# Four w_out rows per partition in one transfer: a change to how the sixteen DMA engines share a weight matrix

## The chip, the core and the metric

The kernel runs on one core of one Trainium2 chip. The metric is the device time of one execution in microseconds (us); before the change it is 663.49 us, the median of three runs (663.15 to 664.74). One core has a matrix engine (TensorE, "PE" in the profile, with its weight loads as "PEld"), a vector engine (VectorE, "DVE"), an activation engine (ScalarE, "ACT"), GpSimd ("POOL"), and SyncE ("SP"), which here only issues transfers. Sixteen DMA engines move data between the chip's memory and the core's 128-partition scratch memory. Each of the computing engines works through its own instructions in order and waits on semaphores for the others.

## What is computed

One decoding step with four sequences, in bf16: attention over a key and value cache, and a small gated MLP (gMLP) beside it, added together.

```python
x, xn = A_x, layernorm(A_x)                      # x: (4, 1, 640)
q = (xn @ wq) per head                           # 32 heads of 128, 4096 cached positions
o = softmax(q @ k_cache^T * 128**-0.5) @ v_cache # k_cache, v_cache: (4, 32, 4096, 128)
z = gelu(xn @ w_in)                              # w_in: (640, 1728)
z1, z2 = z[..., :864], layernorm(z[..., 864:])
g = w_sp @ z2 + b_sp                             # one position: two scalars
out = x + o @ wo + (z1 * g) @ w_out              # wo: (4096, 640), w_out: (864, 640)
```

The two caches are 134 MB each. Of the 282.6 MB that the kernel moves, w_out is 864 rows of 1,280 bytes, 1.1 MB.

## The kernel before

**Memory.** One large buffer `kv` is cut into five slots of SL = 16,384 bf16 elements per partition (32 KB). A unit of cache (all positions of eight heads of one sequence) is 64 KB per partition, 8 MB in all, and takes two neighbouring slots; sixteen units of K and sixteen of V go through the five slots. `place` says which two: K0 goes to slots 3 and 4, K1 to 0 and 1, K2 to 2 and 3, K3 to 4 and 0, V0 to 1 and 2. Before the cache comes, the same slots hold other things: slot 0 holds wq and the layernorm's scratch, slot 2 everything of the gMLP.

Slot 2 is filled from its start in this order (elements per partition): w_in (8,640), the first FA rows per partition of w_out (FA x 640), the float32 array `z_f` (3,840 elements' room), the bf16 array `z_b` (1,280), and `I4`, a 128x128 float32 matrix of ones and zeros (256 elements' room). With FA = 3 they end at 8,640 + 1,920 + 3,840 + 1,280 + 256 = 15,936, inside the slot.

**The rest of w_out.** What `w_out` doesn't hold goes into `w_words` (DVE clears it first, L128), as three pieces (`PC`): 20, 12 and 8 partitions with several rows each. SP issues the first two, POOL the third, behind a small transfer into a tile `walk` that nothing reads. A piece's partitions are dealt out to 5, 3 and 2 DMA engines, four partitions to each. `w_words` is used again later: `kT_t`, the two buffers into which DVE transposes the keys, lies over the same words.

**Order of the transfers.** SP issues nearly all of them, in program order: wq, w_in, w_out (L126, L127), two pieces (L133), K0, K1, K2, K3 (in halves), then V and K in turns (L181). An issue waits until its slots are free. After the last V come the rows of wo that were left (L189), the last in five cuts.

**The gMLP's chain.** After the layernorm of x, PE computes the queries and z (L338, L339 for the rows in `w_out`, L343 for the pieces), ACT applies gelu, and a chain of small steps runs over all engines: DVE sums (L371, L373), PE spreads the sums with `I4` (L376), then L378, L380, L382, L385, L386, L387, L388, L389, a transpose on DVE (L390), and 40 matmuls with w_out on PE (L403), in twenty chunks of two halves. `I4` is written by POOL at L235, and L376 is its only reader.

**The keys.** `emit_K` transposes an eighth of a K unit on DVE (L425) into one of the two buffers and multiplies it on PE (L436). In the order of DVE, K0's transposes stand behind L390. In the order of the source, the issue of K0's transfer (`load_unit(seq[0])`) stands ahead of the copy at L235. A framework places the waits: each instruction waits for the earlier ones, transfers included, that touch the same bytes, and the framework also sets the order within an engine.

Of the kernel before, what the change touches and what calls it, by code (L numbers as in the profile page):

```python
# [16 lines left out]
def kernel(  # L17
# [19 lines left out]
    nc = tc.nc  # L37
    P = 128
# [3 lines left out]
    DC = D // P  # L42
# [9 lines left out]
    NG = H // HG  # L52
# [1 line left out]
    G = HG * B  # L54
    F2 = B_w_in.shape[1]
    Fh = F2 // 2
    FA = 3
    FR = 17
    nf = FA * P

    PC = ((0, 20, 10, 5), (32, 44, 12, 3), (60, 68, 17, 2))
    f_at = [nf]
    for p0, p1, n, _ in PC:
        f_at.append(f_at[-1] + (p1 - p0) * n)
    assert Fh == f_at[-1]
    FC = FA + FR
    NOUT = A_wo.shape[1]
# [18 lines left out]
    def misc_ps(shape, dtype):  # L86
        misc_ctr[0] += 1
        return ps_m.tile(shape, dtype, tag="misc", name=f"misc{misc_ctr[0]}")
# [5 lines left out]
    n_p = (2 * TC + 1) * 16  # L94
    w_words = const.tile([P, max(2 * NKT + n_p, FR * NOUT // 2)], F32, name="w_words")
    kT_t = w_words[:, 0:2 * NKT].rearrange("p (i n) -> p i n", i=2)
    pT_t = w_words[:, 2 * NKT:2 * NKT + n_p].bitcast(BF16).rearrange("p (j r) -> p j r", r=32)

    def at_slot(i, n, off=0):
        return kv[:, i * SL + off:i * SL + off + n]  # L100
# [22 lines left out]

    w_out = at_slot(2, FA * NOUT, n_in).rearrange("p (c n) -> p c n", c=FA)

    nc.sync.dma_start(out=w_out[:, 0:2], in_=B_w_out[0:2 * P, :].rearrange("(p c) n -> p c n", p=P))  # L126
    nc.sync.dma_start(out=w_out[:, 2:3], in_=B_w_out[2 * P:nf, :].rearrange("(p c) n -> p c n", p=P))  # L127
    nc.vector.memset(w_words[:, 0:FR * NOUT // 2], 0.0)  # L128
    w_rest = w_words[:, 0:FR * NOUT // 2].bitcast(BF16).rearrange("p (c n) -> p c n", c=FR)

    def load_piece(eng, t):
        p0, p1, n, k = PC[t]
        return eng.dma_start(out=w_rest[p0:p1, 0:n].rearrange("p c n -> p (c n)"),  # L133
                             in_=B_w_out[f_at[t]:f_at[t + 1], :].rearrange("(r i c) n -> i r (c n)", i=k, c=n))
# [10 lines left out]
    NB = 32 * FC  # L145
    z_at = n_in + FA * NOUT

# [26 lines left out]
    def load_unit(item):  # L174
        key, u = item
        g, b = divmod(u, B)
        cache = A_k_cache if key == "k" else A_v_cache
        src = cache[b, g * HG:(g + 1) * HG].rearrange("e (m t) d -> (e m) (t d)", t=T)
        c = cuts.get(item, (0, T))
        for t0, t1 in zip(c[:-1], c[1:]):  # L180
            nc.sync.dma_start(out=unit(item, t0, t1), in_=src[:, t0 * Dh:t1 * Dh])  # L181
# [5 lines left out]
    def load_wo(g, c_cuts=(0, HG)):  # L187
        for c0, c1 in zip(c_cuts[:-1], c_cuts[1:]):
            nc.sync.dma_start(out=wo_t[g][:, c0:c1, :], in_=wo_q[g][:, c0:c1, :])  # L189
# [30 lines left out]
    xnT = const.tile([P, DC, 32], BF16)  # L220
# [43 lines left out]
    for q in range(4):  # L264
        nc.gpsimd.tensor_copy(out=SelE[32 * q:32 * q + 32, :, q % 2, :],
                              in_=b8[32 * q:32 * q + 32, 8:8 + HP, None].to_broadcast((32, HP, P // HG)))
# [10 lines left out]
                          in_=ident_f[:].rearrange("p (q x c) -> p q x c", q=2, c=C2))  # L277
# [12 lines left out]
    for hf in range(NH):  # L290
        nc.tensor.matmul(proj[0:32, 0:NO2], lhsT=ident_bf[:XR, 1 - hf:33 - hf],
                         rhs=x_bf[:, hf * NO2:(hf + 1) * NO2], start=(hf == 0), stop=False)
# [4 lines left out]
    for hf in range(2):  # L297
        for c in range(DC):
            for j in range(NG):
                n0 = j * HG * Dh + hf * 512  # L300
                nc.tensor.matmul(q4_ps[32 * j:32 * j + 32, hf * 512:hf * 512 + 512], lhsT=xnT[:, c, :],  # L301
                                 rhs=wq[:, c, n0:n0 + 512], start=(c == 0), stop=(c == DC - 1))
# [14 lines left out]
    w_z = w_in.rearrange("p c (a f) -> p c a f", a=2)  # L317
    z_ps = misc_ps([P, 2, FA, 32], F32)
    zr_ps = misc_ps([P, 2, 256], F32)


    z_in = [[], [], [], []]
    for t, (p0, p1, n, k) in enumerate(PC):
        src = w_z[:, :, :, f_at[t]:f_at[t + 1]]
        for q in range(p0 // 32, (p1 - 1) // 32 + 1):
# [5 lines left out]
                src_q = src  # L331
            z_in[q].append((t, x0 - 32 * q, x1 - 32 * q, src_q))
    z_of = [[sum((x1 - x0) * PC[t][2] for t, x0, x1, _ in z[:m]) for m in range(len(z) + 1)] for z in z_in]
    w_z2 = w_z[:, :, :, 0:2 * P].rearrange("p c a (q j i) -> p c q a i j", q=4, j=32)
    w_z1 = w_z[:, :, :, 2 * P:nf].rearrange("p c a (q j) -> p c q a j", q=4)
    for c in range(DC):
        for q in range(4):
            nc.tensor.matmul(z_ps[32 * q:32 * q + 32, :, 0:2], lhsT=xnT[:, c, :], rhs=w_z2[:, c, q], start=(c == 0), stop=False)  # L338
            nc.tensor.matmul(z_ps[32 * q:32 * q + 32, :, 2], lhsT=xnT[:, c, :], rhs=w_z1[:, c, q], start=False,  # L339
                             stop=(c == DC - 1))  # L340
        for q in range(4):
            for m, (_, _, _, src) in enumerate(z_in[q]):
                nc.tensor.matmul(zr_ps[32 * q:32 * q + 32, :, z_of[q][m]:z_of[q][m + 1]], lhsT=xnT[:, c, :], rhs=src[:, c],  # L343
                                 start=(c == 0 and m == 0), stop=(c == DC - 1 and m == len(z_in[q]) - 1))
# [3 lines left out]
    nc.gpsimd.memset(z_f[:, 0:2, :], 0.0)  # L348
    nc.scalar.activation(out=zT[:, :, 0:FA, :], in_=z_ps[:], func=ACT.Gelu_apprx_tanh)
    for q in range(4):  # L350
        rows = slice(32 * q, 32 * q + 32)
        for m, (t, x0, x1, _) in enumerate(z_in[q]):
            p0, p1, n, k = PC[t]
            z = zr_ps[rows, :, z_of[q][m]:z_of[q][m + 1]]
# [3 lines left out]
            else:  # L358
                for a in range(2):
                    nc.scalar.activation(out=dst[:, a].rearrange("p c (i r) -> p c i r", i=k),  # L360
                                         in_=z[:, a].rearrange("p (r i c) -> p c i r", i=k, c=n), func=ACT.Gelu_apprx_tanh)
# [36 lines left out]
    for f0 in range(0, FC, 4):  # L398
        for hf in range(NH):
            for fc in range(f0, min(f0 + 4, FC)):  # L400
# [3 lines left out]
                                 rhs=(w_out[:, fc] if fc < FA else w_rest[:, fc - FA])[:, hf * NO2:(hf + 1) * NO2],  # L404
                                 start=(fc == 1 and hf == 0), stop=False)
# [11 lines left out]
    def emit_K(u, k):  # L417

        g, b = divmod(u, B)
        hh = first.get(u, 0) ^ (k // 4)  # L420
        qp, kh = k // 2 % 2, k % 2
        t0 = 2 * TC * (2 * hh + qp)
        kw = unit(("k", u), t0, t0 + 2 * TC).bitcast(F32).rearrange("p (t w) -> p t w", w=KW)[:, :, 32 * kh:32 * kh + 32]
        kT = kT_t[:, k % 2]
        nc.vector.transpose(kT.rearrange("p (t r) -> p t r", r=32), kw)  # L425
        if ("S", g) not in state:
            S_new = ps_s.tile([P, 2, TC, M], F32, tag="S", name="S")
            state[("S", g)] = S_new
        S_ps = state[("S", g)]
        kb = kT.bitcast(BF16).rearrange("p (i t e m w) -> p i t e m w", i=2, e=NE, m=M, w=2)  # L430
        w0 = 8 - (b * C2 + hh)
        for w in range(2):
            for i in range(2):
                for e in range(NE):
                    q = 2 * qp + e
                    nc.tensor.matmul(S_ps[32 * q:32 * q + 32, i], lhsT=QZ[:, b, 2 * kh + w, e, w0:w0 + 32],  # L436
                                     rhs=kb[:, i, :, e, :, w], start=(b == 0 and k < 4 and kh == 0 and w == 0),
                                     stop=(b == B - 1 and k >= 4 and kh == 1 and w == 1))
# [89 lines left out]
    def emit_sel(g):  # L528

        ox = misc_ps([P, B, P // HG, HG], F32)  # L530
        nc.tensor.matmul(ox[:].rearrange("p b q c -> p (b q c)"), lhsT=SelX[:].rearrange("p h q -> p (h q)"),  # L531
                         rhs=state["R"][:].rearrange("p b d -> p (b d)"), start=True, stop=True)
        om = ppool.tile([P, B, P // HG, HG], F32, tag="p", name="om")
        nc.vector.tensor_tensor(out=om[:], in0=ox[:], in1=MkQ[:, None, :, None].to_broadcast((P, B, P // HG, HG)), op=ALU.mult)
        state[("om", g)] = om
# [27 lines left out]
    for i, item in enumerate(seq):  # L563
        if i + 1 < len(seq):
            key, u = seq[i + 1]
            load_unit(seq[i + 1])
            if key == "k" and u == 2 * B - 1:
                load_wo(u // B - 1)
        else:
            load_wo(NG - 3)  # L570
            load_wo(NG - 2)
            load_wo(NG - 1, (0, 2, 4, 6, 7, 8))
        key, u = item
        g, b = divmod(u, B)
        if key == "k":
            done = b == B - 1 and g > 0
            for k in range(8):
                emit_K(u, k)
                if done and k == 1:
                    emit_sel(g - 1)  # L580
                if done and k == 2:
                    emit_oT(g - 1)
                if done and k == 5 and g == 1:
                    emit_proj(g - 1)
            if b == B - 1:
                if g < NG - 1:
                    fill_qz(g + 1)
                softmax(g)
        else:
            emit_V(u)  # L590
# [58 lines left out]
```

## Time and profile before

| | |
|---|---|
| median of three runs | 663.49 us (663.15 to 664.74) |
| profiled execution, its own time | 663.36 us |
| span of the profiled execution | 661.6 us |
| DMA rate over the span | 427 GB/s, 282.60 MB in 7276 packets |
| DVE, PE busy | 377.3 us, 281.7 us |
| mean granted TensorE clock | 0.755 of full speed |

The trace lists each DMA packet with queue, start, length and size, but not the DMA engine that moved it. On a busy engine a packet begins about 3 ns before the one ahead of it ends, and every engine moves the same sequence of sizes, so the packets fall into sixteen chains. Packets of 12,800 bytes (first piece) appear on five chains, of 15,360 (second) on three of these five, of 21,760 (third) on two others. Eighteen packets of 16,384 bytes of the queue that the page calls "q8 instruction" go to eight further chains in turn, two or three to each; every one takes 1.07 us and draws out a neighbouring packet by about 0.5 us. One chain has neither. By these chains, in us from the span's start:

| chains | K0's share has landed | K1's share has landed | last share of wo has landed |
|---|---|---|---|
| three, both pieces of SP | 45.07, 45.48, 45.51 | 64.40, 64.80, 64.86 | 658.48, 658.03, 658.24 |
| two, first piece only | 42.90, 42.90 | 62.21, 62.22 | 656.29, 658.42 |
| two, POOL's piece | 44.32, 44.41 | 63.64, 63.73 | 656.93, 657.01 |
| six with two instruction packets | 40.70 to 41.07 | 60.02 to 60.39 | 656.49 to 656.82 |
| two with three instruction packets | 40.99, 42.27 | 60.31, 61.63 | 658.07, 658.28 |
| the one left | 42.15 | 61.47 | 654.85 |

Five of the sixteen, the ones with SP's pieces, also show six gaps of 0.30 us, each with a long packet behind it; between the first packet at 2.2 us and the last share of wo no other engine has a gap over 0.05 us.

How to read the answers below: times are us from the span's start; "out<-in" names the tiles; `x8` is a count; a bracket says how long the engine had been idle and who ended it.

### The profile page before, as it was taken

What the parts mean: (1) busy time and instruction counts of PE and PEld (TensorE: products, weight loads), DVE (VectorE), ACT (ScalarE), POOL (GpSimd) and SP (SyncE); (2) the same over time, 40 slices, a digit from 0 to 9 for tenths busy, and PEclk for the clock granted to TensorE, in tenths of its full rate; (3) what the DMA queues carried; (4) which work ended last, traced back from release to release, by engine and by line L of the source; (5) the groups of instructions that cost most, each with busy time, mean ns of one, the idle gap of its engine ahead of it and who ended that gap; (6) DMA issues with size and microseconds to landing.
All of it is one profiled execution on the core that took longest, in us unless ns stands there. A gap on an engine that the chain in (4) does not pass through costs nothing.

```text
span 661.6 us, 5513 instructions
## 1 busy us (share of the span) xinstructions
PE 281.7 (43%) x2293; PEld 106.9 (16%) x2293; DVE 377.3 (57%) x307; ACT 73.9 (11%) x143; POOL 70.3 (11%) x138
## 2 busy tenths in 40 slices
PE   0445555437052455334435075532606245652236
PEld 0221111112011121111112021110202112120012
DVE  4329989766191758718346196864629175971112
ACT  0300000330100000340200000070110000043200
POOL 3620000030200000130300000030020000003300
PEclk9868879778687697677759677875867778666779
DMA  8999999999999999999999999999999999999997
GB/s 367 458 421 440 425 436 445 436 421 440 421 436 437 444 405 436 441 441 436 433 420 428 437 422 445 442 425 432 432 433 432 433 440 411 446 432 429 423 423 286
DMA packets 7276, 282.60 MB, mean 427 GB/s; under 512 B 929, under 2 KB 1324, under 8 KB 1836
## 3 DMA queue, kind: packets, MB, share of 16 engines
q1 hardware_dynamic: 7112, 282.07, 98.9%
q8 instruction: 18, 0.29, 0.2%
q0 software_dynamic: 112, 0.18, 0.1%
q14 instruction: 6, 0.05, 0.0%
q10 hardware_dynamic: 28, 0.01, 0.0%
HBM read 282.25 MB, written 0.01 MB: 427 GB/s over the span
## 4 chain that ended last, share of the span: by engine, by line
DMA 74%; DVE 12%; issue 11%; PE 2%; ACT 0%; SPq 0%; DVEq 0%; ACTq 0%
DMA kv<-in_A_k_cache_dram 63%; DVE w_words L425 11%; DMA kv<-in_A_v_cache_dram 5%; DMA kv<-in_A_wo_dram 3%; DMA kv<-in_A_wq_dram 3%; PE O L509 1%; DVE w_words L491 0%; PE S L436 0%; DVE Zb L469 0%; DVE m L443 0%; PE last L552 0%; ACT p_bf L485 0%; SPq L189 0%; PE proj L552 0%; PE misc L447 0%
## 5 line engine op out<-in xcount | busy, mean ns | idle before, releaser
L425 DVE STREAM_TRANSPOSE w_words<-kv 128x2048 f32<-128x2048 f32 x128 | 282.8, 2275 | 127.2 <-DMA kv<-in_A_k_cache_dram 127.2
L436 PE MATMUL S<-w_words,QZ 128*32 128x512 bf16 x1024 | 183.3, 490 | 262.5 <-DVE w_words L425 262.5
L436 PEld LDWEIGHTS <-QZ 128*32 128x32 bf16 x1024 | 59.2, 110 | 384.3 <-issue 318.1
L509 PE MATMUL O<-kv,Zb 128*32 128x512 bf16 x1024 | 72.0, 443 | 57.6 <-DMA kv<-in_A_v_cache_dram 51.1
L473 ACT ACTIVATE Zb<-w_words,MkE 32x128 bf16<-32x128 bf16 x120 | 60.9, 508 | 117.2 <-PE O L509 103.3
L518 DVE TENSOR_TENSOR om<-O,Mk 128x512 f32<-128x512 f32 x15 | 10.4, 692 | 92.1 <-PE O L509 92.1
L471 POOL TENSOR_SCALAR Zb<-w_words,MkE 32x128 bf16<-32x128 bf16 x60 | 43.3, 722 | 138.6 <-PE O L509 118.0
L485 ACT ACTIVATE p_bf<-S,negmax 128x1024 bf16<-128x1024 f32 x4 | 4.5, 1114 | 401.5 <-DVE negmax L453 401.5
L509 PEld LDWEIGHTS <-Zb 128*32 128x32 bf16 x1024 | 33.3, 110 | 96.1 <-issue 66.5
L469 DVE TENSOR_SCALAR Zb<-w_words,MkE 32x128 bf16<-32x128 bf16 x76 | 24.9, 327 | 2.3
L411 POOL COPY QZ<-qT 32x32 bf16<-32x32 bf16 x16 | 5.0, 315 | 184.9 <-PE S L436 184.3
L519 DVE TENSOR_REDUCE R<-om 128x128 f32<-128x512 f32 x15 | 15.3, 1020 | 0.5
L496 POOL TENSOR_SCALAR rs<-MkB,rowsum 128x4 f32<-128x4 f32 x4 | 1.2, 296 | 112.2 <-ACT p_bf L485 112.2
L491 DVE STREAM_TRANSPOSE w_words<-p_bf 128x1024 bf16<-128x1024 bf16 (+1 forms) x8 | 9.6, 1240 | 5.9 <-ACT p_bf L485 4.1
L542 POOL MEMSET oT<- 128x66 bf16 x4 | 0.5, 146 | 98.0 <-PE proj L552 98.0
L443 DVE TENSOR_REDUCE m<-S 128x1 f32<-128x1024 f32 x4 | 4.9, 1224 | 6.1 <-PE S L436 6.1
L521 DVE TENSOR_SCALAR R<-O,Mk 128x128 f32<-128x128 f32 x1 | 0.4, 351 | 13.0 <-PE O L509 13.0
L531 PE MATMUL misc<-R,SelX 128*128 128x512 f32 x8 | 4.5, 644 | 7.2 <-DVE R L519 5.5
L301 PE MATMUL q<-kv,xnT 128*32 128x512 bf16 x40 | 4.5, 631 | 6.4 <-DVE xnT L222 6.4
L498 PE MATMUL misc<-rs,SelE 128*128 128x4 f32 x8 | 2.3, 364 | 10.4 <-POOL rs L496 10.4
L552 PE MATMUL proj<-kv,oT 128*8 128x320 bf16 x52 | 5.6, 352 | 1.2 <-DMA kv<-in_A_wo_dram 1.2
L128 DVE MEMSET w_words<- 128x5440 f32 x1 | 4.6, 4592 | 1.9 <-issue 1.9
(107 smaller groups left out, 87.9 us busy)
## 6 DMA issues: line engine op xcount, KB each, us to landing
kv<-in_A_k_cache_dram SPq DMA_DIRECT2D x8, 4096.0 KB, 30.2
kv<-in_A_v_cache_dram SPq DMA_DIRECT2D x1, 6144.0 KB, 28.6
kv<-in_A_wq_dram SPq DMA_DIRECT2D x1, 5120.0 KB, 17.2
kv<-in_A_wo_dram SPq DMA_DIRECT2D x3, 1280.0 KB
kv<-in_B_w_in_dram SPq DMA_DIRECT2D x1, 2160.0 KB, 22.7
kv<-in_A_v_cache_dram SPq DMA_DIRECT2D x1, 2048.0 KB
kv<-in_A_wo_dram SPq DMA_DIRECT2D x3, 320.0 KB, 22.7
kv<-in_B_w_out_dram SPq DMA_DIRECT2D x1, 320.0 KB, 23.0
```

Of the source, the lines that this page charges most:

```text
L411: nc.gpsimd.tensor_copy(out=QZ[r0:r0 + 32, :, :, :, 8 + 8 * hp], in_=qT[32 * g:32 * g + 32, NE * hp:NE * hp + NE].rearrange("p e a b -> p ...
L425: nc.vector.transpose(kT.rearrange("p (t r) -> p t r", r=32), kw)
L436: nc.tensor.matmul(S_ps[32 * q:32 * q + 32, i], lhsT=QZ[:, b, 2 * kh + w, e, w0:w0 + 32], rhs=kb[:, i, :, e, :, w], start=(b == 0 and k < ...
L443: nc.vector.tensor_reduce(out=m1[:], in_=S_ps[:].rearrange("p i t m -> p (i t m)"), axis=AX.X, op=ALU.max)
L469: nc.vector.tensor_scalar(out=dst, in0=src, scalar1=mk, scalar2=None, op0=ALU.mult)
L471: nc.gpsimd.tensor_scalar(out=dst, in0=src, scalar1=mk, scalar2=None, op0=ALU.mult)
L473: nc.scalar.activation(out=dst, in_=src, func=ACT.Copy, scale=mk)
L491: nc.vector.transpose(pT_t[:, j0:j1, :], blocks)
L509: nc.tensor.matmul(O_ps[32 * q:32 * q + 32, :, :], lhsT=Zb[b % 2][:, w].rearrange("p h c -> p (h c)"), rhs=vv[:, w * 4 * Dh:(w + 1) * 4 * ...
L518: nc.vector.tensor_tensor(out=om4[:], in0=O_ps[:], in1=Mk4[:, :, None].to_broadcast((P, 4, Dh)), op=ALU.mult)
L519: nc.vector.tensor_reduce(out=R, in_=om4[:].rearrange("p c d -> p d c"), axis=AX.X, op=ALU.add)
L552: nc.tensor.matmul(dst[0:nb, 0:n1 - n0], lhsT=state[("oT", g)][:, c0:c0 + nb], rhs=wo_t[g][:, c, n0:n1], start=start, stop=stop)
```

## The change

FA goes from 3 to 4 and FR from 17 to 16, so `w_out` takes 512 rows, four per partition, in one transfer instead of two, and the pieces have 4, 12 and 16 rows per partition instead of 10, 12 and 17. All else that counts in FA follows: `w_out` is 2,560 elements per partition instead of 1,920, so `z_f`, `z_b` and `I4` begin 640 elements further on, and the end of `I4` is at 16,576. The z matmuls for the rows in `w_out` are one per chunk of x and quarter instead of two. The second to last tile of wo is loaded in two halves.

```diff
-    FA = 3
-    FR = 17
+    FA = 4
+    FR = 16
...
-    PC = ((0, 20, 10, 5), (32, 44, 12, 3), (60, 68, 17, 2))
+    PC = ((0, 20, 4, 5), (32, 44, 12, 3), (60, 68, 16, 2))
...
-    nc.sync.dma_start(out=w_out[:, 0:2], in_=B_w_out[0:2 * P, :].rearrange("(p c) n -> p c n", p=P))
-    nc.sync.dma_start(out=w_out[:, 2:3], in_=B_w_out[2 * P:nf, :].rearrange("(p c) n -> p c n", p=P))
+    nc.sync.dma_start(out=w_out, in_=B_w_out[0:nf, :].rearrange("(p c) n -> p c n", p=P))
...
-    w_z2 = w_z[:, :, :, 0:2 * P].rearrange("p c a (q j i) -> p c q a i j", q=4, j=32)
-    w_z1 = w_z[:, :, :, 2 * P:nf].rearrange("p c a (q j) -> p c q a j", q=4)
+    w_za = w_z[:, :, :, 0:nf].rearrange("p c a (q j i) -> p c q a i j", q=4, j=32)
     for c in range(DC):
         for q in range(4):
-            nc.tensor.matmul(z_ps[32 * q:32 * q + 32, :, 0:2], lhsT=xnT[:, c, :], rhs=w_z2[:, c, q], start=(c == 0), stop=False)
-            nc.tensor.matmul(z_ps[32 * q:32 * q + 32, :, 2], lhsT=xnT[:, c, :], rhs=w_z1[:, c, q], start=False,
-                             stop=(c == DC - 1))
+            nc.tensor.matmul(z_ps[32 * q:32 * q + 32], lhsT=xnT[:, c, :], rhs=w_za[:, c, q], start=(c == 0), stop=(c == DC - 1))
...
             load_wo(NG - 3)
-            load_wo(NG - 2)
+            load_wo(NG - 2, (0, 4, 8))
             load_wo(NG - 1, (0, 2, 4, 6, 7, 8))
```

## The prediction

> **What bounds the kernel now.** I read the slices of the page first, then the chain of waits, then the opening of the timeline, SP's waits and the packet records.
>
> ```profile
> DMA  8999999999999999999999999999999999999997
> DMA kv<-in_A_k_cache_dram 63%; DVE w_words L425 11%; DMA kv<-in_A_v_cache_dram 5%; DMA kv<-in_A_wo_dram 3%; DMA kv<-in_A_wq_dram 3%; PE O L509 1%; DVE w_words L491 0%; PE S L436 0%; DVE Zb L469 0%; DVE m L443 0%; PE last L552 0%; ACT p_bf L485 0%; SPq L189 0%; PE proj L552 0%; PE misc L447 0%
> ```
>
> The DMA engines are busy in every slice, and the chain is mostly DMA. The sixteen chains of packets have no idle time to speak of between 2.2 us and the last wo share, so the span is the packet time of the slowest DMA engine (its last share lands at 658.48) plus a tail of 661.57 - 658.48 = 3.09 us for the last matmuls, the sum and the store. A change can thus act in two ways: through the bytes of the slowest engine, or by letting the queues run dry. The second asks when each transfer is issued:
>
> ```profile
> 17.95 27.57 DMA kv<-in_A_k_cache_dram
> 45.52 0.03 issue
> ...
> 52.36 2.28 DVE w_words L425
> 54.64 0.02 SPq L181
> 54.66 0.04 issue
> 54.70 0.03 SPq L181
> 54.73 0.03 issue
> 54.76 29.46 DMA kv<-in_A_k_cache_dram
> ```
>
> In this stretch of the chain K0 lands at 45.52, DVE transposes its first half, which frees slot 3, and only then, at 54.7, does SP issue K2. The engines are done with K1 between 60.02 and 64.86, so K2 comes 5.3 us ahead of the first to need it. This margin, less the start of a transfer, is all the cover the opening has.
>
> ```profile
> 16.34 0.45 POOL L235 COPY kv<-I 128x128 f32<-128x128 f32 x1
> ...
> 29.80 0.82 DVE L373 TENSOR_REDUCE st_in<-kv 128x1 f32<-128x640 f32 x1 [0.51 <-POOL kv L372]
> 30.67 0.50 PEld L376 LDWEIGHTS misc<-st_in,kv 128*128 128x128 f32 x2 [5.18 <-DVE st_in L373]
> ...
> 37.77 0.85 DVE L390 STREAM_TRANSPOSE kv<-kv 128x640 bf16<-128x640 bf16 x1 [5.33 <-POOL kv L389]
> 38.67 4.85 PEld L403 LDWEIGHTS <-kv 128*8 128x8 bf16 x40 [7.50 <-DVE kv L390]
> ...
> 39.46 4.41 PE L403 MATMUL proj<-w_words,kv 128*8 128x320 bf16 x33
> ...
> 45.74 17.66 DVE L425 STREAM_TRANSPOSE w_words<-kv 128x2048 f32<-128x2048 f32 x8 [7.12 <-DMA kv<-in_A_k_cache_dram]
> ```
>
> The timeline of the opening: the gMLP's chain is over at 43.87, and DVE then waits for K0 with nothing left before it. So the gMLP is hidden, by 45.74 - 43.87 = 1.9 us.
>
> **The change, part by part.**
>
> *Rows and packets.* From the records: a packet of 10,240 bytes costs 385.5 ns, of 2,560 bytes 99, of 1,280 bytes 52; a line between the first two gives 194 for 5,120 (estimate). All engines: w_out was 8 x 99 + 8 x 52 + 12 (two closing packets of 6) = 1,220 ns, becomes 8 x 194 + 6 = 1,558, +0.34 us. The five with the first piece: four packets of 12,800 (476 ns) become 5,120: -1.13, net -0.79. The two with POOL's piece: 21,760 (805 ns) to 20,480, -0.19, net +0.15. The split of wo's second to last tile: 16 x 194 + 12 against 8 x 385.5 + 6, +0.03 for all. If nothing else happened, the three would end at 657.7, the slowest instruction-loaded engine at 658.28 + 0.37 = 658.65, the new end: +0.2 us.
>
> *Fewer z matmuls, a shorter DVE clear, one issue less on SP.* PE drops 20 matmuls and 20 weight loads of L338 and L339, which all lie between 23.9 and 25.4, under the wait for K0; SP's extra issue (0.92 us) was over before the first packet; the clear shrinks by 6% of 4.6 us and holds back only the pieces. Nothing, as long as the wait for K0 is there. One more DMA issue for wo (0.3 us on SP) has 13 us of queued data in front of it.
>
> *I4 leaves its slot.* It now lies from 16,320 to 16,576, and the slot ends at 16,384: 192 of its 256 elements are slot 3's first, where K0 goes. K0's transfer is issued ahead of the copy in the source, so the copy must wait for it. The built order of the changed kernel says so: the copy's only wait is for the second count of the semaphore that K0's transfer raises, and the framework has put it on POOL behind the copies of the queries and the squares (L372), ahead of L380. K1's issue still waits for the copy of the queries alone, so it keeps its time. The 192 elements of K0 are then read with I4's content in them: a matter of values, not of time.
>
> So L376 starts not at 30.67 but after K0 has landed. K0 lands with its slowest engine, now 45.5 - 0.79 = 44.7 us. Copy: 44.7 + 0.06 + 0.45 = 45.2. From the end of L373 (30.62) to the first matmul of L403 (38.67) are 8.05 us, unchanged steps: 53.3. POOL's steps behind the copy, DVE's L378 to L390 and, behind them, all of K0's transposes wait in line. K0's first transpose also writes words that w_out's pieces hold; in the built order it waits for the 22nd of the 40 matmuls (before too, but then that was long past). 40 took 5.2 us: 22 take 2.9 at the same clock, so 56.1 against 45.74. Four transposes take 54.64 - 45.74 = 8.9: K2 is issued at 65.0, 10.3 us later.
>
> By then every DMA engine has run dry (K1 ends between 60.3 and 64.1, the rows counted). From issue to first packet with empty queues: wq 1.46 us (0.72 to 2.18), the stores at the end 1.23; I take 1.35, so K2 starts at 66.35 on all sixteen at once. The Trainium skill, "DMA: Bandwidth & Descriptors", section "Latency and other measured facts", gives about 0.6 us to the first byte on this path; with SP's 0.33 us of issue that would make 65.9 and the sum 0.4 us less, and the rows above say more.
>
> A restart may cost: the first packets of wq took 1.53 to 2.74 us for 1.51. Bounds 0 and 1.2, I take 0.4, since these queues were empty for 2 to 6 us and not from the start.
>
> From K1's end to its last share an engine needed: without instruction packets or gaps 593.3 (656.93 - 63.64), with two instruction packets 596.45 (656.74 - 60.29), with three 597.76 (658.07 - 60.31). All now start together, so the heaviest ends last. The eighteenth instruction packet came at 656.4, 70 PE instructions before the end; with 40 fewer in the program it comes 40 later, among the last 30, probably as the data run out: I take 596.45 + 0.03. Sum: 66.35 + 0.4 + 596.5 = 663.25, plus the tail 3.09 = 666.35, against 661.57 in the same execution: **+4.8 us**. The median shown stands 0.13 above that execution's own time, so 663.49 + 4.8 = **668.3 us**.
>
> *What is late next.* DVE runs K0 to K3 without a pause from 56.1, 17.6 us each, to 126.7 (119.6 before). V0's issue: K2's first half, 100.3, wanted by 66.75 + 38.7 - 1.35 = 104.1. K4: K3's first half, 118.0, wanted by 123.4. V1, which waits for most of V0's matmuls: 133.52 - 119.61 = 13.9 behind K3, so 140.6, wanted by 66.75 + 4 x 19.35 - 1.35 = 142.8. Each keeps 2 us or more; a second hole isn't expected.
>
> **Rivals.**
> 1. *The hole closes: not slower.* The mechanism is K2's margin: if K2 is issued by 59.0 no queue is empty and only the balance is left, 663.49 + 0.2 = **663.7**. For that the chain from K0's landing to K0's fourth transpose must take 14.3 us and not 20.3. The bare durations inside it can't give this: 8.9 are DVE at work, 8.05 the small steps, so even with matmuls at no cost it is 17.5. It would need the copy to pass before K0 has landed. I give 6%. Faster than 661.5 would need a lighter slowest engine beside that: 2%.
> 2. *A late instruction packet.* If the eighteenth falls into an engine's last share, 597.76 holds: +1.3, **669.6**. 22%.
> 3. *A second hole at V1.* Should DVE or the softmax lose more than 2.2 us, V1 is late and all engines wait again; at 4 us lost, 1.8 more: **670.1**. Nothing in these rows takes that long: 8%.
> 4. *Matmuls at the full clock.* L436's eight take 1.89 us at half and 1.12 at full clock; were L403's to halve, K0 starts 1.3 earlier and the hole shrinks by as much: **667.0**. 17%.
>
> **How the numbers follow.** The forecast itself has 45%. Around it: matmul clock -1.3, K0's landing -0.4, restart -0.4 to +0.8, instruction packet +1.3, a gap of the kind seen on five engines +0.6. The range 666.3 to 670.4 takes these in, and rivals 2, 3 and 4 with them. About 0.3%, 2 us, is what a measurement of this kernel can tell from no change: slower has 92% (forecast and rivals 2, 3, 4), no change 6% (rival 1), faster 2%.
>
> **What would show it.** The copy of I4 on POOL at 45 and not at 16; L376 at 45; the first transpose of K0 near 56; SP's issue of K2 near 65; the DMA share of 60 to 66 falling from about 1 to under a half. If the copy stands before 40, or the DMA share stays whole up to 70, the forecast is wrong. If the balance alone counted, the last wo share would land near 658.6 and nothing in the opening would move.

## The result, and the profile after

The changed kernel takes 669.34 us (median of six runs, 669.15 to 670.73) against 664.33 us beside it (six runs, 663.15 to 664.74); the ratio is 1.0087, with an interval of 1.0077 to 1.0097. Some of the runs of the kernel before take 664.2 to 664.7 and the others 663.2 to 663.5; here four of its six were of the longer kind, and the quotient of the two medians is 1.0075. Beside the experiments the median of the kernel before was 663.3 to 663.4, and the loss 5.9 us. The forecast was 668.3, +4.8 us.

First the page of the changed kernel: DMA share and rate in forty slices of 16.7 us, and the lines of the chain.

```profile
DMA  9997899999999999999999999999999999999996
GB/s 371 447 428 322 388 433 443 436 412 428 439 428 439 435 409 452 431 433 435 436 435 431 420 423 430 449 436 427 436 428 435 436 431 413 455 435 436 414 415 271
DMA kv<-in_A_k_cache_dram 60%; DVE w_words L421 12%; DMA kv<-in_A_v_cache_dram 9%; DMA kv<-in_A_wo_dram 1%; PE O L505 1%; DVE w_words L127 1%; PE proj L399 0%; POOL kv L383 0%; SPq L132 0%; POOL kv L385 0%; POOL kv L384 0%; DVE kv L386 0%; PE misc L372 0%; DVEq L421 0%; SPq L180 0%
```

One place differs: the fourth slice, 50 to 67 us, moves 322 GB/s where the neighbouring ones move 388 and 428. From the sixth slice to the last but one the rates are 409 to 455 GB/s (before: 405 to 446), and the gMLP's steps (L383 to L386, L399), which were hidden, are now in the chain. Its start, in order of time (start, length, what):

```profile
8.00 36.93 DMA kv<-in_A_k_cache_dram
44.98 0.30 POOL kv L234
45.32 0.60 PE misc L372 x2
...
52.41 0.86 DVE kv L386
53.31 3.14 PE proj L399 x22
56.47 2.37 DVE w_words L421 x2
```

K0 lands, POOL copies I4 (L234 here, L235 before) at 44.98 instead of 16.34, the gMLP's steps follow one another, and K0's first transpose waits until the 22nd matmul with w_out is through. K0's issue itself moved from 17.95 to 8.00, which the prediction doesn't name: before, SP waited 9.6 us there for wq's transfer. It moves nothing else, since the DMA engines are still busy with the weights; K0's first packets are recorded from 20.94 on before and from 21.25 on after.

SP's issue of K2 (the line puts it together with the next one, of K3's first half) and the DMA share of the stretch that follows (timeline, then windows; a window has its length, the busy time and count of PE, PEld, DVE, ACT and POOL, and in the last three columns granted clock, DMA share and GB/s):

```profile
65.49 9.00 SPq L180 DMA_DIRECT2D kv<-in_A_k_cache_dram  x2
```

```profile
50.00:55.00 5.00, 1.69 (x14) 1.02 (x16) 0.84 (x1) 0.00 (x0) 2.29 (x2) 0.50 0.97 419
55.00:60.00 5.00, 3.97 (x38) 2.09 (x34) 3.53 (x2) 0.00 (x0) 0.00 (x0) 0.83 0.99 423
60.00:65.00 5.00, 2.79 (x16) 0.88 (x16) 5.00 (x3) 0.00 (x0) 0.00 (x0) 0.85 0.15 66
65.00:70.00 5.00, 3.10 (x18) 1.02 (x20) 5.00 (x4) 0.00 (x0) 0.00 (x0) 0.81 1.03 393
```

The third of these windows in the kernel before:

```profile
60.00:65.00 5.00, 2.42 (x18) 0.77 (x16) 3.41 (x3) 0.00 (x0) 0.00 (x0) 1.00 0.97 419
```

K2 is issued at 65.49 (before: 54.7). Between 60 and 65 the sixteen DMA engines are busy for 15% of the time, where before they were for 97%. DVE works through the whole of it: it isn't waiting, it is late.

**Packet times.** The times taken from packet records (the table of chains, the first packets and last shares of the prediction and the expectations, and those below unless they are called recorded) stand 0.44 us later than the records themselves. Set so, the last share of K0 in the kernel before ends with the rise of its semaphore (45.51 and 45.52), while the records end it at 45.07; the sixteen rises come 0.34 to 0.47 us behind the recorded ends. Differences between packet times aren't touched by this, and in the prediction's sum the 0.44 us of K2's start and of the tail cancel. A time from an issue to a first packet is 0.44 us too long: by the records it is 1.02 us for wq, not 1.46, and 0.79 us for the stores, not 1.23. A time from an issue to the moment when an engine runs dry is too long by as much: K2's 5.3 us were 4.9. The views, the windows among them, go by the records.

### The profile page after: what moved, and what is told of

It reads as the page before. It is cut to its first block, busy times and chain, and to the rows that moved or that the text cites. A ratio compares the mean times of both kernels' runs of the same rounds, so it can differ in the third digit from the quotient of the medians.

```text
span 668.9 us, 5474 instructions
## 1 busy us (share of the span) xinstructions
PE 285.5 (43%) x2273; PEld 108.4 (16%) x2273; DVE 376.6 (56%) x307; ACT 73.7 (11%) x143; POOL 70.0 (10%) x138
## 4 chain that ended last, share of the span: by engine, by line
DMA 70%; issue 13%; DVE 13%; PE 2%; POOL 1%; SPq 0%; DVEq 0%; ACT 0%; POOLq 0%
DMA kv<-in_A_k_cache_dram 60%; DVE w_words L421 12%; DMA kv<-in_A_v_cache_dram 9%; DMA kv<-in_A_wo_dram 1%; PE O L505 1%; DVE w_words L127 1%; PE proj L399 0%; POOL kv L383 0%; SPq L132 0%; POOL kv L385 0%; POOL kv L384 0%; DVE kv L386 0%; PE misc L372 0%; DVEq L421 0%; SPq L180 0%
## 5 line engine op out<-in xcount | busy, mean ns | idle before, releaser
L505 PE MATMUL O<-kv,Zb 128*32 128x512 bf16 x1024 | 74.4, 455 | 58.1 <-DMA kv<-in_A_v_cache_dram 50.9
L372 PE MATMUL misc<-st_in,kv 128*128 128x2 f32 x2 | 0.6, 362 | 17.8 <-POOL kv L234 17.8
```

The lines of the kernel that those rows point to most:

```text
L505: nc.tensor.matmul(O_ps[32 * q:32 * q + 32, :, :], lhsT=Zb[b % 2][:, w].rearrange("p h c -> p (h c)"), rhs=vv[:, w * 4 * Dh:(w + 1) * 4 * ...
```

## The experiments

Each "before" is the median of the kernel before beside that run on one chip.

**I4 in a tile of its own** (changed kernel).

```diff
-    I4 = at_slot(2, 256, z_at + 8 * NB).bitcast(F32).rearrange("p (q k) -> p q k", q=4)
+    I4_t = const.tile([P, P], F32)
+    I4 = I4_t[:].rearrange("p (q k) -> p q k", q=4)
```

> The changed kernel with I4 in a tile of its own instead of the end of slot 2; rows, packets and the split of wo as changed. Wait theory (the 5 us come from I4's wait for K0): the copy is back near 16 us, L372 near 31, K2 is issued near 54.5, no queue runs dry, and only the balance of the rows is left: 0.2 us over the kernel before, about 664.5 (663.8 to 665.2). Rival, rows theory (the new packets and the new shares of w_out cost it): stays at 669.3.

Measured: 663.59 us (before 663.29; ratio 1.0000, 0.9991 to 1.0010). That is below the expected range, which was reckoned from 664.33 for the kernel before; over the kernel before beside it, the medians give 0.3 us for the expected 0.2. K2's issue, from SP's timeline:

```profile
54.14 9.00 SPq L180 DMA_DIRECT2D kv<-in_A_k_cache_dram  x2
```

The loss is gone with the rows, packets and cuts of the change in place. By the medians they cost 0.3 us, which this measurement doesn't tell from nothing.

**I4 in slot 3, nothing else changed** (kernel before).

```diff
-    I4 = at_slot(2, 256, z_at + 8 * NB).bitcast(F32).rearrange("p (q k) -> p q k", q=4)
+    I4 = at_slot(2, 256, z_at + 8 * NB + NOUT).bitcast(F32).rearrange("p (q k) -> p q k", q=4)
```

> The kernel before with one edit: I4 begins 640 elements further on, so that 192 of its 256 elements per partition lie in slot 3, as in the changed kernel; rows and packets as before. As in the changed kernel, K0's transposes then read I4's content in these 192 elements. Wait theory: the whole loss appears, and 0.6 us more than in the changed kernel, since K0's slowest engine still carries the larger pieces and K0 lands at 45.5 instead of 44.9: about 669.9 (669.2 to 670.8). Rows theory: 664.3, nothing moved.

Measured: 671.32 us (before 663.29; ratio 1.0118, 1.0103 to 1.0133). The timeline of POOL and SP:

```profile
45.59 0.29 POOL L235 COPY kv<-I 128x128 f32<-128x128 f32 x1 [15.35 <-DMA kv<-in_A_k_cache_dram]
```

```profile
66.10 0.33 SPq L181 DMA_DIRECT2D kv<-in_A_k_cache_dram  x1
```

The overlap alone makes the loss: copy and K2's issue come 0.6 us after those of the profile above (44.98 and 65.49), as expected, since K0's slowest engine here still carries the larger pieces. But the time lies over the expected range: the loss is 8.0 us where the changed kernel's is 5.9, 2.1 us more and not 0.6. That remainder is the subject of the last experiment.

**K0 cut in halves, so that I4's wait ends sooner** (changed kernel).

```diff
+    cuts[("k", 0)] = (0, T // 2, T)
```

> The changed kernel with K0's transfer cut in two halves. I4 still overlaps slot 3 and overwrites 192 elements of K0 there, but it waits for the first half alone, which lands near 34.6 instead of 44.9. Wait theory: L372 near 35, the first transpose of K0 near 46.1, K2 issued near 55.1, before the queues run dry: about 664.6 (663.9 to 665.4), although the overlap, the rows and the packets are those of the changed kernel. Rows theory: 669.3. A theory that the overlap itself costs (two writers of one place): 669.3 too.

Measured: 663.60 us (before 663.29; ratio 1.0003, 0.9994 to 1.0013), below the expected range for the same reason as with I4 in its own tile: 0.3 us over the kernel before. The copy, from POOL's timeline, and K2's issue, from SP's:

```profile
35.12 0.29 POOL L235 COPY kv<-I 128x128 f32<-128x128 f32 x1 [4.98 <-DMA kv<-in_A_k_cache_dram]
```

```profile
55.63 9.00 SPq L181 DMA_DIRECT2D kv<-in_A_k_cache_dram  x2
```

The copy still waits for a transfer into slot 3, and it costs nothing that can be told. What costs is when the wait ends.

**K0 cut at seven eighths** (changed kernel): `cuts[("k", 0)] = (0, 224, T)`.

> The changed kernel with K0's transfer cut at seven eighths; I4 waits for the first piece, and overwrites its 192 elements as in the changed kernel. A dose between the half cut (663.6) and the whole (669.1): the first piece lands near 41.9 instead of 44.9, so L372, the first transpose (53.4) and K2's issue (62.4) each come 3 us earlier. Wait theory: the engines that carry the end start K2 at 64 instead of 67, so 3 us less than the changed kernel, about 666.1 (665.4 to 666.7). A theory of a step (a missed turn in some queue, that is either there or not) would give 663.6 or 669.1.

Measured: 666.84 us (before 663.34; ratio 1.0049, 1.0034 to 1.0064).

```profile
42.50 0.29 POOL L235 COPY kv<-I 128x128 f32<-128x128 f32 x1 [12.03 <-DMA kv<-in_A_k_cache_dram]
```

The piece landed at 42.5, not 41.9: the copy came 2.3 us sooner than in the changed kernel's second profile (44.79), K2's issue 2.3 us sooner (63.02 against 65.31), the time was 2.43 us less (669.27). The loss comes in doses, not as a step: one us of delay is about one us of time, once the queues are dry. The time lies 0.14 us over the expected range, which fits the landing that was 0.6 us later than expected.

**K2 cut in halves** (changed kernel): `cuts[("k", 2)] = (0, T // 2, T)`.

> The changed kernel (I4's wait kept, with the 192 elements of K0 that it overwrites) with K2's transfer cut in two halves: the first goes to slot 2, which is free when L399 is through (58.4), before the queues run dry at 60.2; the second to slot 3 as soon as K0's first half is transposed (65.5). Theory K2 (the loss is made by K2's late issue alone): the hole at 60 to 67 closes, 664.5 to 665. Theory DVE (the loss is DVE's late start on K0; the transfers behind it are only issued at its pace): the hole moves. DVE still starts at 56.5 and works through K0 to K3 without a pause, so V0 is issued at 100.5 where the engines are dry from 98.9, and V1 at 141 to 142.4 where they are dry at 141.3: the gain is 0.5 us at most, about 668.9 (668.2 to 669.5). My prediction named only the first hole; by its own times for V0, K4 and V1 it must come out as theory DVE.

Measured: 668.10 us (before 663.29; ratio 1.0070, 1.0055 to 1.0085), a loss of 4.8 us: 1.1 us less than the changed kernel, where theory DVE allowed 0.5 us at most, and 0.1 us under its range. Windows of this run:

```profile
60.00:65.00 5.00, 3.00 (x16) 0.95 (x16) 5.00 (x3) 0.00 (x0) 0.00 (x0) 0.77 1.02 439
95.00:100.00 5.00, 3.23 (x20) 0.94 (x17) 5.00 (x3) 0.00 (x0) 0.00 (x0) 0.81 0.86 369
140.00:145.00 5.00, 2.56 (x36) 1.01 (x28) 3.67 (x7) 4.75 (x11) 4.08 (x6) 0.84 0.62 210
```

The hole at 60 is closed, and two others have opened: before V0 (eleven packet chains empty for 0.6 to 3.6 us near 101) and before V1 (0.7 to 2.7 us near 143, on all sixteen). DVE starts on K0 at 56.21 here too and works 32 transposes without a pause, and the issues of V0 (100.21) and V1 (141.74) stay where they were. K2's late issue is only the first place at which DVE's lateness meets an empty queue. Closing it left 4.8 of the 5.9 us, so theory K2 is refuted, and theory DVE holds with a gain that was put too low.

**The changed kernel again, and with V1 cut in halves.** The first profiled execution was the slowest of its six (670.73 us, the others 669.15 to 669.61), and in it the first packets of V1 came up to 1.8 us late or were up to 1.9 us longer than usual on several engines. Is that second hole part of the loss? The cut: `cuts[("v", 1)] = (0, T // 2, T)`.

> The changed kernel unaltered, for a second profile beside the kernel before on one chip. The first profiled execution took 670.73 us and the others 669.2 to 669.6; in it V1 was issued at 142.37, 2.5 us before the first DMA engine needed it, and its first packets came late on several. If that second hole is the odd 1.4 us of that one execution, a profile near 669.3 shows V1 issued about a microsecond earlier and its first packets on time; if it is always there, the same picture with the same hole, and the odd 1.4 us lie elsewhere. 5.8 us over the kernel before, about 669.1.

> The changed kernel, I4's wait and its overwritten 192 elements kept, with V1's transfer cut in two halves: the first, to slot 0, needs only K3's second half transposed (near 127) and is issued well before the engines want it (144.9). It takes away a second hole at V1 and nothing else. If that hole is in every execution: 1 to 1.4 us less than the changed kernel, 667.7 to 668.1. If it was in the profiled one alone: no change, 669.1 (668.7 to 669.4).

Measured: unaltered 669.27 us (ratio 1.0090, 1.0073 to 1.0107), with V1 cut 669.27 us (1.0086, 1.0071 to 1.0101), before 663.34. V1's issue in the first and the second profile of the same kernel:

```profile
142.37 0.33 SPq L180 DMA_DIRECT2D kv<-in_A_v_cache_dram  x1
```

```profile
141.43 0.33 SPq L180 DMA_DIRECT2D kv<-in_A_v_cache_dram  x1
```

In the second, 0.94 us earlier, V1's packets came without a gap. The second hole belongs to that one execution; taking it away changes nothing in the median. Where the 0.94 us come from stands in the timelines of PE and DVE. K0's first transpose was 0.18 us later in the first profile (56.47 for 56.29). The last eight matmuls with K3's keys, which V0's softmax waits for, took 0.68 us more there:

```profile
126.82 1.80 PE L432 MATMUL S<-w_words,QZ 128*32 128x512 bf16 x8 [0.55 <-DVE w_words L421]
```

```profile
126.64 1.12 PE L432 MATMUL S<-w_words,QZ 128*32 128x512 bf16 x8 [1.08 <-DVE w_words L421]
```

Between 126 and 128 the granted clock was 0.50 in the first profile and 1.00 in the second. The last 0.09 us are V0's matmuls (6.01 for 5.92 us).

**K0's transfer behind I4's reader** (changed kernel): the line `load_unit(seq[0])` is moved to just after L372, so no value of K0 is lost.

> The changed kernel with the issue of K0's transfer put in the source behind L372, the only reader of I4, so that no value of K0 is overwritten; now K0's transfer waits for L372 instead of the copy for K0's transfer. Wait theory: L372 is over at 31.3, K0 is issued at 31.4 instead of 18 and starts at 32.8, while the engines are done with the weights between 21.6 and 25: the hole is 8 to 11 us and comes at the front. From there an engine with two instruction packets needs 635.1 (656.74 - 21.65): 32.8 + 0.65 + 635.1 + 3.1 = 671.7 of span, 10 us over the kernel before, about 673.4 (672.4 to 674.4). No second hole: DVE's transposes begin 8 us behind those of the kernel before and the transfers 11. Should K0's issue be hidden, 663.6.

Measured: 675.63 us (before 663.34; ratio 1.0181, 1.0166 to 1.0197), 2.2 us over the expected time and outside its range. SP's timeline and the windows:

```profile
31.44 51.75 SPq L180 DMA_DIRECT2D kv<-in_A_k_cache_dram  x5
```

```profile
20.00:25.00 5.00, 4.04 (x63) 2.17 (x56) 1.72 (x2) 0.58 (x1) 4.39 (x18) 1.00 0.49 205
25.00:30.00 5.00, 0.90 (x12) 0.45 (x6) 1.30 (x4) 4.06 (x9) 2.80 (x6) 0.90 0.00 2
30.00:32.00 2.00, 0.59 (x2) 0.50 (x2) 1.01 (x3) 0.00 (x0) 0.19 (x1) 0.50 0.00 0
```

The place is right: K0 is issued at 31.44, and no DMA engine moves any of the data from 25 to 32.8 (recorded: 24.75 to 32.42). The size was wrong in the weight of the heaviest engine. I took one with two instruction packets (635.1 us from here); the first of the eighteen came at 43.4, behind the hole, so the engine that takes the first, the ninth and the seventeenth (645.4) had all three behind it, and such an engine needs 636.8 (658.28 - 21.51, before). The eighteenth came at 669.9, when at most one engine still had data to load. With the 0.7 us by which the first packets of K0 lengthened (33.0 + 0.7 + 636.8) the last share lands at 670.5; it landed at 670.35.

**Two z matmuls instead of one** (changed kernel), to give PE its 40 instructions back.

```diff
-            nc.tensor.matmul(z_ps[32 * q:32 * q + 32], lhsT=xnT[:, c, :], rhs=w_za[:, c, q], start=(c == 0), stop=(c == DC - 1))
+            for h in range(2):
+                nc.tensor.matmul(z_ps[32 * q:32 * q + 32, :, 2 * h:2 * h + 2], lhsT=xnT[:, c, :], rhs=w_za[:, c, q][:, :, 2 * h:2 * h + 2],
+                                 start=(c == 0 and h == 0), stop=(c == DC - 1 and h == 1))
```

> The changed kernel with each z matmul for w_out's rows cut in two again (20 matmuls and 20 weight loads more, under the wait for K0, as in the kernel before); I4's wait and the 192 elements that it overwrites stay. It asks why the kernel before with I4 in slot 3 lost 2.0 us more than the changed kernel, where K0's later landing explains 0.6. Theory of the eighteenth instruction packet: with 40 more PE instructions it comes 40 instructions sooner, at 662 instead of 664 to 665, while the engine that moves it still has its last shares to load; that engine then carries three packets behind the hole and the others two: 1.3 to 1.5 us over the changed kernel, 670.6 (670.2 to 671.0). If PE's program has no part in it (the larger pieces, the smaller packets of w_out): 669.2.

Measured: 670.67 us (before 663.41; ratio 1.0105, 1.0088 to 1.0122), 1.4 us over the changed kernel. In its packet records the last instruction packet comes at 662.2, its engine's last share lands at 665.66, and no other engine's after 664.4; in the second profile of the changed kernel it comes at 664.0, and the last share lands at 664.20. The end of the chain of waits, first in this run and then in that profile:

```profile
640.23 24.60 DMA kv<-in_A_wo_dram
664.83 0.04 issue
664.88 1.27 PE last L550 x16
```

```profile
654.75 9.44 DMA kv<-in_A_wo_dram
664.19 0.04 issue
664.23 0.32 PE last L548 x4
```

So twenty matmuls and weight loads that nobody waits for cost 1.4 us, through the place of one 16 KB packet. The kernel before with I4 in slot 3 has as many PE instructions: its last instruction packet comes at 662.6, and its engine ends at 666.40, the others by 664.9. By these records that is the remainder there: 2.1 us, less the 0.6 to 0.8 us by which K2's issue is later than in the changed kernel's two profiles (66.10 against 65.49 and 65.31).

## Why the prediction was right, and where it was small

The mechanism is shown from both sides: without the overlap the loss is gone (663.59), and the overlap alone makes it (671.32). Step by step, with the second profile of the changed kernel (span 667.3), which has no second hole:

| step | predicted | measured |
|---|---|---|
| copy of I4 | 44.8 to 45.2 | 44.79 |
| first transpose of K0 | 56.1 | 56.29 |
| K2 issued | 65.0 | 65.31 |
| K2's first packets begin | 66.35 | 66.72 to 67.59 (recorded: 66.28 to 67.14) |
| their extra length | 0.4 | 0.1 to 1.3, mean 0.7 |
| last share of wo landed | 663.25 | 664.20 |

- *The waits* (K0's landing, copy, small steps, 22 matmuls, four transposes) came out within 0.3 us; the 22 matmuls took 3.14 us in the first profile, mostly at a granted clock of 0.50, for my 2.9.
- *The restart was mis-sized.* I took "1.35" from issue to first packet and "0.4" for the lengthening. In the same packet times the sixteen first packets began 1.4 to 2.3 us after the issue, 1.6 on average, and were 0.7 us longer on average. Together with K2's 0.3 us this is the 0.9 us by which the end was late. By the records the first packets began 0.97 to 1.83 us after the issue began, 1.18 on average. The Trainium skill's 0.6 us to the first byte ("DMA: Bandwidth & Descriptors", "Latency and other measured facts") agrees with the earliest of the sixteen, which is recorded 0.64 us behind SP's 0.33 us of issue; the average is 0.2 us more. So the prediction's remark that the rows say 0.4 us more than the skill is wrong: that difference is the 0.44 us by which its packet times stand late.
- *The remaining data.* The sum's 596.5 us from K2's start was right: the second packets of K2 began at 70.07 on average, one usual packet (2.41) behind a start at 67.66, and 67.66 + 596.5 = 664.16 against 664.20.
- *Rows and packets.* Put at +0.2 us if nothing else happened; measured +0.30 by medians, not told from zero. One reading beside it was wrong without a consequence: SP's extra issue in the kernel before ended at 3.04, not before the first packet (2.2, recorded 1.74).
- *What is late next.* The margins held: V0, K4 and V1 were issued at 100.30, 117.84 and 141.43 for my 100.3, 118.0 and 140.6. V1 is the late one, by 0.8 us: V0's matmuls took 5.92 us, where those of the kernel before, from which the 13.9 us were taken, took 4.99. And V1's 2.2 us was no safe margin: in the first profiled execution V1 was 1.8 us later than predicted, and the hole was there.

The rivals: the closed hole (1) is refuted by the DMA share of 0.15. The late instruction packet (2) didn't strike the changed kernel, but its price is real: it strikes as soon as PE has 40 instructions more, and cost 1.4 us for the 1.3 forecast. The second hole (3) was there in the first of two profiled executions, and the medians with V1 whole and cut are equal. The full matmul clock (4) didn't come: the window from 50 to 55 has 0.50.

Not tried: a version that takes advantage of the lighter engines. With I4 in its own tile the shares are as the change meant them, and the time is that of the kernel before.

## What to carry to other kernels

When a size grows inside a hand-packed region, work out where the last tenant ends: an overlap of 384 bytes with the next region turned into a wait for an 8 MB transfer. A wait that lands on a hidden chain costs nothing until what stands in line behind it, on the same engine, is what frees the buffers; then compare the time at which the next transfer is issued with the time at which the queues run dry. Past that point the loss follows one for one (the copy at 44.79 and 42.50 gave 5.9 and 3.5 us), before it there is next to none (35.12: 0.3 us), and closing the first hole only shows the next one if the late engine has no slack to catch up.

The wait also hides an error. It sets an order between K0's transfer and the copy, but both still write the same 384 bytes of each partition, and the copy comes last: the changed kernel takes I4's ones and zeros for keys there. With I4 in a tile of its own both the wait and the error are gone.

## What the runs showed of the hardware

- The program's own instructions are loaded by the same DMA engines as the data, 18 packets of 16 KB on eight of the sixteen. Each takes 1.07 us and draws a neighbour out by 0.5 us. In this kernel, which keeps all DMA engines busy, they count as load, and the place of the last one, set by the length of PE's program, moved the end by 1.4 us.
- While the queues are never empty, unequal shares keep the DMA engines apart: in the kernel before they were up to 4.8 us apart at K1's end. The hole before K2 set them all to nearly one start (recorded 66.28 to 67.14 in the second profile), so a balance reached by unequal shares ahead of it is lost, and the end is made by the heaviest engine of what remains.
- An 8 MB transfer issued 2.1 us before the first engine ran dry by the records (142.37 for 144.47) came late on several engines in one execution; issued 2.9 us before (141.43 for 144.36) it came on time. Why 2.1 us weren't enough, where the first packets of K2 began 0.97 to 1.83 us after their issue, no run shows.
- The granted clock differs between executions of one program at the same place: the same eight matmuls took 1.80 us at 0.50 and 1.12 us at 1.00, and this moved the issue of V1 by 0.68 us.
